# One transformer block with adaptive LayerNorm: TensorE's order in the four query blocks given as a list of 4188 single decisions instead of thirteen rules named by a table

## The chip, the cores and the metric

The kernel runs on one core of a Trainium2 chip. Its time is the device time of one execution in microseconds (us). A core has five engines, each with its own list of instructions that it works through in order: TensorE (PE in the profile, with PEld for the loading of its weights), VectorE (DVE), ScalarE (ACT), GpSimd (POOL) and SyncE (SP), which here issues the DMAs. An engine waits where an operand isn't there yet or where the buffer that it is to write is still being read.

## The reference

One transformer block over 2048 tokens of width 576, in float32: a conditioning vector gives six vectors that scale, shift and gate two LayerNorms and their branches; attention has 32 heads of 18, the MLP a hidden width of 4608.

```python
mod = (_silu(c) @ w_mod).reshape(c.shape[0], 6, 1, -1)
sa, ca, ga, sb, cb, gb = (mod[:, 0], mod[:, 1], mod[:, 2], mod[:, 3], mod[:, 4], mod[:, 5])
h = _layernorm(x, axis=-1) * (1 + ca) + sa
x = x + ga * _A_ref(h, A_wqkv, A_wo)
h = _layernorm(x, axis=-1) * (1 + cb) + sb
x = x + gb * _B_ref(h, B_w1, B_w2)
...
scores = jnp.einsum("bhqd,bhkd->bhqk", q, k) * (Dh ** -0.5)
p = _softmax(scores, axis=-1)
o = jnp.einsum("bhqk,bhkd->bhqd", p, v)
...
h = _silu(jnp.einsum("bsd,df->bsf", x, w1))
out = jnp.einsum("bsf,fd->bsd", h, w2)
```

## The kernel before, in words

**Stages.** A first part (up to some 155 us of the span) normalizes x, transposes it and computes all values and the first queries and keys. Then come four blocks of 512 queries. A block goes through the 32 heads in eight groups of four ("quads"), a quad through 16 tiles of 128 keys. What follows the attention of a block (output projection, second LayerNorm, the MLP) is computed while the next block's attention runs; that of the last block stands alone at the end (the tail).

**Three kinds of steps.** TensorE's order between the first part and the tail is a sequence of steps of three kinds, and the whole change is about that sequence:

- A *score step* (`s`, slot_a L835 and slot_b L865) is two matmuls of 512 columns that use one half of the array's rows each and run side by side. `psa` (L831, q·k with the queries in the rows) serves for the maximum of each row of scores: DVE reduces it (`mx`, L833). `psb` (L883, k·q with the keys in the rows) belongs to a place 40 slots earlier, whose maximum is known by then; ACT takes its exp into a tile `pt` (L885). Three banks of PSUM serve `psa` (and one more that it may borrow from the filler as long as the MLP isn't open), three `psb` in block 0 and two later. A bank is free again when DVE or ACT has read it.
- A *value step* (`1` to `4`, run_pv L905, pv L913) multiplies the exps of one to four tiles of keys with the values. A tile of keys is four matmuls (one for each head), each on 32 columns of the array, and each goes through the array in two passes, so that the profile shows 8 records of L920 for one tile. All 16 tiles of a quad add up in the one bank `psv`; then ACT copies it out (`ov`, L924), DVE transposes and divides by the sums (L938 to L943), and DMAs bring it to `ou` (L948). Nine `pt` pairs exist, so scores can run only so far ahead of the values.
- A *filler step* (`f`, Filler L287) is a piece of other work. In block 0 it is five (or four) matmuls over all 128 rows that compute the rest of the queries and keys (`psqk`, L612), then the filler list is empty until the block's attention is done. Then, for the block that has just ended: the projection (`psp`, from the split copies `th` and `tl` of `ou`, L1007 to L1012), the LayerNorm, the transposes `psT` (L1071), and the MLP, where `w1t` goes with `hh`/`hl` (mlp1, L1141) and `w2t` with `g` (mlp2, L1174). These are float32 products made of parts (hi·hi, hi·lo, lo·hi), split into pairs of half-row matmuls (L499); in the tail they go over all rows (L493). Between mlp1 and mlp2 stand ACT's tanh (L1167), DVE (L1168), ACT's `g` (L1170) and POOL's low part of `g` (L1171).

So the array is used in three shapes: half rows, all rows, 32 columns.

**The end of a block.** The projection of a block may start when its last quad's values are out, transposed, moved by DMA and split (`th`). The last group of mlp2 of the MLP that runs beside it (the last four of the 36 hidden tiles, `left` in the code) is kept back to be done there.

**What sets the order.** A planner (Plan, L113) follows the kernel while it is built: it has a clock `plan.t`, adds the cost of each step of TensorE (a score step TS, a tile of values TV, TX for a change of the array's shape, L93), and works off queues for DVE and ACT with their durations, so that it knows at each point which banks would be free. The main loop (L1613) asks at each point which kinds of step would be ready by that plan, and takes one of them by nine numbers (how far the filler may be ahead or behind its pace, how many tiles of values are collected, how loaded DVE must be, ...). Thirteen such rules have letters (WAYS, L61), and a table of letters (TABLE, L77) names one for every six half slots. Where no step is taken, the plan's clock moves on by 20 ns. All decisions fall when the kernel is built; the chip gets a fixed list. What the steps issue on SP (loads of `ka`, `kb`, `qt`, `vt`, of weights, stores) is issued with the step; weights of block 0's MLP are loaded raw, split by POOL (L720 to L724) and stored, paced by the plan's clock (serve, L733). The order on DVE, ACT and POOL is set by a scheduler that works from the same program.

Of the kernel before, what the change touches and what calls it, by code (L numbers as in the profile page):

```python
# [39 lines left out]
LEAD = 40  # L40
# [20 lines left out]
WAYS = {  # L61
# [13 lines left out]
}  # L75
SPAN = 6
TABLE = (  # L77
    "aaaaaaaaaaaaaaaaaaaaaaakaaaakgaaaaakaaaaaaaaaaaaaaaaaaaamaaaaaaaaaacaaaaaaaaakaaaaaaaaaaaaaaaaaaaaad"
    "aggaaaggaaaaaaaaaaaaaaaaaaaaaaaaaaaaaaaaaaaaaaaaaaaaaaaaaaaaaaaaaaaaaaaaaaaaaaaaaaaaaaaaaaaaaeaaaamd"
    "afaaaaaaaaaaaaaaaaaafaaaaacaaaaamaaaaaaaaaaaaaaaaaaaaaaaaaaaaaaaaaaafmalaaaafammfaada"  # L80
# [12 lines left out]
TS, TV, TX, TL, TR = 229, 862, 112, 430, 60  # L93
# [260 lines left out]
def tile_adaln_block(ctx: ExitStack, tc: tile.TileContext, x, wqkv, wo, w1, w2, c, wfirst, wcol, out):  # L354
# [1257 lines left out]
    stood = 0  # L1612
    while now < 2 * (total + LEAD) or pend or later:  # L1613
# [8 lines left out]
        more = now < 2 * (total + LEAD)  # L1622
        n = kts_ready()
        room = state["p"] + (now % 2 == 0) <= len(pts)
        scores = more and room and plan.is_ready(plan.when("b")) and (plan.is_ready(plan.when("a")) or may_borrow())
        work = fill.pos < len(fill.items)
        AHEAD, KEEP, NEAR, LOADED, LOADED2, NEXT, STAND, PVMAX, PVMIN = WAYS[TABLE[min(now // SPAN, len(TABLE) - 1)]]
        target = fill.target() if work else now + AHEAD - 1
        ahead = now - target
        busy = work and fill.ready()  # L1630
        if n >= PVMAX or n and more and not room and (ahead < 0 or not busy):
            do = "v"
        elif "p" not in mp:

            if busy and plan.mode != "half" and ahead > -NEXT and plan.backlog("V") >= LOADED2:
                do = "f"
            elif scores and ahead < AHEAD:
                do = "s"
# [99 lines left out]
```

## Time and profile before

| | us |
|---|---|
| three runs: median (lowest to highest) | 2374.59 (2371.91 to 2375.4) |
| the profiled execution | 2372.1 |
| its span, first to last instruction | 2370.3 |
| block 0: first psb to first psp | 155.6 to 569.2 |
| block 1: first psp to first psp of the next | 569.2 to 1105.0 |
| block 2 | 1105.0 to 1615.1 |
| block 3, up to its first psp | 1615.1 to 2108.3 |
| tail, to the end of the span | 2108.3 to 2370.3 |

The mean granted clock of TensorE is 0.991 of full speed. In the profile a group has its source line, engine, operation and tiles (out<-in), the number of instructions, their busy time and mean duration, and the idle time of the engine before them with what ended it. Rows in order of time have start, duration, the same names, and idle time in brackets.

### The profile page before, as it was taken

The page shows a single profiled execution, that of the slowest core. Times are in us where ns is not written, and L with a number is a line of the kernel's source. Part 1 is how long each engine was busy: PE and PEld are TensorE (multiplying, and loading weights), DVE is VectorE, ACT ScalarE, POOL GpSimd, SP SyncE. Part 2 cuts the span into 40 slices and gives each one's busy share as a digit, 9 for nine tenths or more (in the row PEclk, how much of TensorE's full clock was granted, in tenths as well). Part 3 has the DMA queues.
Part 4 walks back from the last instruction along what each step waited for, and adds up shares of the span by engine and source line. Part 5 has one row for each costly group of instructions (what it writes and reads, how often), then busy time and mean ns, then how long its engine had stood idle before and what let it go on. Part 6 is the DMA issues. An engine that isn't in the chain of part 4 may idle for free.

```text
span 2370.3 us, 52177 instructions
## 1 busy us (share of the span) xinstructions
PE 2301.3 (97%) x19844; PEld 1576.1 (66%) x19844; DVE 1775.2 (75%) x3089; ACT 1476.4 (62%) x2710; POOL 710.1 (30%) x873
## 2 busy tenths in 40 slices
PE   5999999999999999999999999999999999989999
PEld 4874444445566677666667776766666777678998
DVE  7768989887888888777888878887888888144333
ACT  4237777775677777666777777775777777712121
POOL 5104333316656666664211111122211111110000
PEclk9999999999999999999999999999999999999999
DMA  7455546546656666665655445554545554335653
GB/s 248 158 184 177 177 155 175 176 161 198 207 181 219 214 215 215 215 211 177 227 168 178 165 165 180 175 187 143 192 163 189 179 188 155 113 138 205 217 204 115
DMA packets 201475, 433.02 MB, mean 183 GB/s; under 512 B 31362, under 2 KB 67618, under 8 KB 201226
## 3 DMA queue, kind: packets, MB, share of 16 engines
q1 hardware_dynamic: 201226, 429.68, 54.6%
q8 instruction: 159, 2.61, 0.5%
q14 instruction: 90, 0.74, 0.1%
HBM read 338.54 MB, written 86.33 MB: 179 GB/s over the span
## 4 chain that ended last, share of the span: by engine, by line
PE 85%; DVE 6%; DMA 3%; POOL 2%; ACT 1%; issue 1%; SPq 0%; DVEq 0%; ACTq 0%; POOLq 0%
PE ps L499 25%; PE psv L920 18%; PE psa L831 13%; PE ps L493 10%; PE psb L883 8%; PE psqk L612 4%; DVE mx L833 3%; PE psv L499 2%; PE psp L499 1%; DMA raw<-in_w 1%; PE psv L1400 1%; PE psqk L499 1%; PE psqk L1400 1%; PE psp L493 1%; DMA kb<-kscr 1%
## 5 line engine op out<-in xcount | busy, mean ns | idle before, releaser
L833 DVE TENSOR_REDUCE mx<-psa 128x1 f32<-128x512 f32 x2048 | 1329.0, 684 | 287.2 <-PE psb L883 164.2
L885 ACT ACTIVATE pt<-psb 128x512 f32<-128x512 f32 x2048 | 1139.9, 599 | 472.9 <-PE psb L883 299.8
L883 PE MATMUL psb<-qt,kb 56*128 56x512 f32 x2048 | 738.9, 421 | 6.4 <-ACT pt L885 5.6
L831 PE MATMUL psa<-ka,qt 54*128 54x512 f32 x2016 | 724.0, 418 | 8.0 <-DVE mx L833 6.3
L831 PEld LDWEIGHTS psa<-ka,qt 54*128 54x128 f32 x2016 | 340.2, 186 | 306.5 <-DVE mx L833 204.9
L920 PE MATMUL psv<-pt,vt 128*32 128x512 f32 x4096 | 509.7, 602 | 0.2 <-ACT ov L924 0.2
L499 PE MATMUL ps<-w2t,g 64*128 64x288 f32 x4992 | 406.2, 294 | 8.5 <-POOL w2t L724 5.7
L499 PEld LDWEIGHTS ps<-w2t,g 64*128 64x128 f32 x4992 | 381.0, 186 | 41.8 <-POOL w2t L724 7.0
L883 PEld LDWEIGHTS psb<-qt,kb 56*128 56x128 f32 x2048 | 346.8, 186 | 35.1 <-ACT pt L885 24.1
L499 PE MATMUL ps<-hh,w1t 64*128 64x512 f32 x1944 | 358.0, 394 | 1.6 <-DVE x L1033 1.5
L1171 POOL TENSOR_TENSOR g<-etmp,g 128x512 fp32r<-128x512 f32 x108 | 137.4, 1292 | 406.3 <-ACT g L1170 298.5
L920 PEld LDWEIGHTS psv<-pt,vt 128*32 128x32 f32 x4096 | 101.0, 109 | 214.7 <-issue 209.4
L499 PEld LDWEIGHTS ps<-hh,w1t 64*128 64x128 f32 x1944 | 196.7, 187 | 45.0 <-DVE mx L833 5.0
L1037 POOL TENSOR_TENSOR x<-x,gt 128x288 f32<-128x288 f32 x116 | 93.0, 802 | 402.0 <-ACT gt L1036 401.5
L499 PE MATMUL ps<-hl,w1t 64*128 64x512 f32 x864 | 179.4, 392 | 0.0
L1033 DVE TENSOR_TENSOR x<-ps,x 128x288 f32<-128x288 f32 x184 | 83.7, 455 | 113.6 <-PE ps L493 76.8
L493 PE MATMUL ps<-w2t,g 128*128 128x288 f32 x960 | 133.2, 299 | 7.4 <-ACT g L1170 5.9
L493 PEld LDWEIGHTS ps<-w2t,g 128*128 128x128 f32 x960 | 130.8, 191 | 9.9 <-ACT g L1170 6.3
L1167 ACT ACTIVATE eq<-ps 128x512 f32<-128x512 f32 x36 | 21.5, 598 | 146.4 <-PE ps L493 146.4
L493 PE MATMUL ps<-hh,w1t 128*128 128x512 f32 x360 | 107.0, 391 | 0.5 <-DVE hh L428 0.5
L499 PEld LDWEIGHTS ps<-hl,w1t 64*128 64x128 f32 x864 | 90.1, 187 | 14.8
L1168 DVE SCALAR_TENSOR_TENSOR etmp<-etmp 128x512 f32<-128x512 f32 x108 | 75.8, 739 | 27.7 <-ACT etmp L1167 27.5
(150 smaller groups left out, 2124.7 us busy)
## 6 DMA issues: line engine op xcount, KB each, us to landing
w1t<-w1s SPq DMA_DIRECT2D x108, 640.0 KB
w2t<-w2s SPq DMA_DIRECT2D x108, 576.0 KB
kb<-kscr SPq DMA_DIRECT2D x512, 108.0 KB
ka<-kscr SPq DMA_DIRECT2D x504, 108.0 KB
w1s<-w1t SPq DMA_DIRECT2D x36, 640.0 KB
w2s<-w2t SPq DMA_DIRECT2D x36, 576.0 KB
vt<-vscr SPq DMA_DIRECT2D x32, 608.0 KB
qt<-qscr SPq DMA_DIRECT2D x128, 108.0 KB
```

The lines of the kernel that those rows point to most:

```text
L493: mm(self.ps[late], lhsT=lhsT, rhs=rhs, start=(i == 0), stop=(i == self.n - 1))
L499: done = mm(self.ps[g], lhsT=lhsT[rows], rhs=rhs[rows], start=(s == 0), stop=(s == self.end))
L612: mm(qk_ps[0], lhsT=w[b][:, kt, :], rhs=(hTl if a else hTh)[:, kt, n * 512:(n + 1) * 512], start=(i == 0), stop=(i == 13))
L831: mm(ps, lhsT=t["q"][64 * j:64 * j + 54, hp, stt * P:(stt + 1) * P], rhs=t["a" if ("a", kc, hp) in t else "b", kc, hp][64 * j:64 * j + 54, ...
L833: return lambda: nc.vector.tensor_reduce(t["mx"][:, 2 * j + hp, stt, kc:kc + 1], ps, axis=AX.X, op=ALU.max)
L883: state["pe"] = mm(ps, lhsT=t["b", kt // 4, hp][64 * e:64 * e + 56, kt % 4 * P:(kt % 4 + 1) * P], rhs=t["q"][64 * e:64 * e + 56, hp, :], s ...
L885: nc.scalar.activation(t["P"][kt, hp][:, e, :], ps, AF.Exp, scale=SCALE)
L920: mm(t["ps"][32 * h:32 * h + 32, :], lhsT=t["v"][:, c0:c0 + 32], rhs=t["P"][kt, h // 2][:, h % 2, :], start=(kt == 0), stop=(kt == NKT - 1 ...
L1033: nc.vector.tensor_add(c["x1"][j][:, hs], ps, c["x1"][j][:, hs])
L1037: nc.gpsimd.tensor_add(c["x1"][j][:, hs], c["x1"][j][:, hs], t)
L1168: nc.vector.scalar_tensor_tensor(t, t, 1.0, u, op0=ALU.add, op1=ALU.mult)
L1171: (nc.vector if last else nc.gpsimd).tensor_tensor(g[:, 1, :], t, f(g[:, 0, :]), op=ALU.subtract)
```

## The change

The table of rules and the thirteen rules go. In their place stands a string with one character for each step: `s`, `f`, or a digit for a value step of so many tiles. The main loop takes the next character and waits, by the plan's clock, until that step is ready by the plan; it never takes another one. The planner's costs for a score step, a tile of values and a change of shape become smaller. The instructions themselves stay what they are.

```diff
-WAYS = {
-    "a": (12, 6, 500, 900, 900, 8, 0, 5, 3),
...
-SPAN = 6
-TABLE = (
-    "aaaaaaaaaaaaaaaaaaaaaaakaaaakgaaaaakaaaaaaaaaaaaaaaaaaaamaaaaaaaaaacaaaaaaaaakaaaaaaaaaaaaaaaaaaaaad"
...
+ORDER = (
+    "sssfsssfsssfsss1sss1sssfsssfsssfss1sss1sss1sss1sss1sss1sss1sss2sssfsssfsssfsss1sss1sss1sss1ss1sssfsss2sssffsss"
...
-TS, TV, TX, TL, TR = 229, 862, 112, 430, 60
+TS, TV, TX, TL, TR = 228, 858, 100, 430, 60
...
         room = state["p"] + (now % 2 == 0) <= len(pts)
-        scores = more and room and plan.is_ready(plan.when("b")) and (plan.is_ready(plan.when("a")) or may_borrow())
-        work = fill.pos < len(fill.items)
-        AHEAD, KEEP, NEAR, LOADED, LOADED2, NEXT, STAND, PVMAX, PVMIN = WAYS[TABLE[min(now // SPAN, len(TABLE) - 1)]]
-        target = fill.target() if work else now + AHEAD - 1
-        ahead = now - target
-        busy = work and fill.ready()
-        if n >= PVMAX or n and more and not room and (ahead < 0 or not busy):
-            do = "v"
...
-        elif n >= PVMIN or n and stood >= STAND:
-            do = "v"
+        do = ORDER[step] if step < len(ORDER) else ""
+        if do == "s":
+            ready_ = room and plan.is_ready(plan.when("b")) and (plan.is_ready(plan.when("a")) or may_borrow())
+        elif do == "f":
+            ready_ = fill.pos < len(fill.items) and fill.ready()
         else:
-            do = None
-        stood = 0 if do else stood + 20
-        if not do:
-            if not more and not pend:
+            ready_ = do and kts_ready() >= int(do)
+        if not ready_:
+            if not do and not pend:
                 run_later(2)
                 state["now"] += 1
                 now += 1
             plan.t += 20
             continue
+        step += 1
```

What this moves on TensorE is shown at three places. The line numbers of the changed kernel are 20 higher: L851 is the `psa` of L831, L903 the `psb` of L883, L940 the values of L920, L519 and L513 the filler of L499 and L493. `psa` and `psb` one after the other are one score step; two rows of `psv` with their x2 are one tile of keys.

The first place is TensorE at the end of block 0, behind the last `psqk`, where there is no filler until the projection. Before:

```order
L920 MATMUL psv_6441<-pt_2034,vt_2040 32x512 x2
L920 MATMUL psv_6441<-pt_2035,vt_2040 32x512 x2
L831 MATMUL psa<-ka_82,qt 128x512
L883 MATMUL psb<-qt,kb_85 128x512
L831 MATMUL psa<-ka_82,qt 128x512
L883 MATMUL psb<-qt,kb_85 128x512
L831 MATMUL psa<-ka_82,qt 128x512
L883 MATMUL psb<-qt,kb_84 128x512
L831 MATMUL psa<-ka_82,qt 128x512
L883 MATMUL psb<-qt,kb_84 128x512
L920 MATMUL psv_6441<-pt_2036,vt_2040 32x512 x2
L920 MATMUL psv_6441<-pt_2037,vt_2040 32x512 x2
```

At the same place in the changed kernel:

```order
L940 MATMUL psv_6475<-pt_2036,vt_2040 32x512 x2
L940 MATMUL psv_6475<-pt_2037,vt_2040 32x512 x2
L851 MATMUL psa<-ka_80,qt 128x512
L903 MATMUL psb<-qt,kb_87 128x512
L851 MATMUL psa<-ka_80,qt 128x512
L903 MATMUL psb<-qt,kb_87 128x512
L940 MATMUL psv_6475<-pt_2038,vt_2040 32x512 x2
L940 MATMUL psv_6475<-pt_2030,vt_2040 32x512 x2
```

Four score steps stood between two tiles of values; now two do, at most of these places, and once twelve. The last `psqk` stands 59 score steps ahead of the first `psp` before, and 47 now.

The second place is TensorE at the end of block 1, behind the last matmuls of mlp1 (`w1t` with `hh`, whose result `g` the first w2t matmul behind it needs). Before:

```order
L499 MATMUL ps_15173<-hh,w1t 128x512
L920 MATMUL psv_15400<-pt_2038,vt_2039 32x512 x2
L920 MATMUL psv_15400<-pt_2030,vt_2039 32x512 x2
L831 MATMUL psa<-ka_83,qt 128x512
L883 MATMUL psb<-qt,kb_86 128x512
L831 MATMUL psa<-ka_83,qt 128x512
L883 MATMUL psb<-qt,kb_86 128x512
L920 MATMUL psv_15400<-pt_2031,vt_2039 32x512 x2
L920 MATMUL psv_15400<-pt_2032,vt_2039 32x512 x2
```

At the same place in the changed kernel:

```order
L519 MATMUL ps_15263<-hh,w1t 128x512
L851 MATMUL psa<-ka_80,qt 128x512
L903 MATMUL psb<-qt,kb_88 128x512
L851 MATMUL psa<-ka_80,qt 128x512
L903 MATMUL psb<-qt,kb_88 128x512
L940 MATMUL psv_15462<-pt_2038,vt_2039 32x512 x2
L940 MATMUL psv_15462<-pt_2030,vt_2039 32x512 x2
L940 MATMUL psv_15462<-pt_2031,vt_2039 32x512 x2
L940 MATMUL psv_15462<-pt_2032,vt_2039 32x512 x2
```

From there to the first w2t matmul stood ten score steps and four tiles of values; now nine score steps and six tiles do. In addition 26 half matmuls of w1t that stood ahead of the block's last value product now stand behind it (54 at the end of block 2).

The third place is TensorE at the end of the last block's attention. Before, the last tile of values stands here, w2t halves follow, then a whole pair of mlp1 (`ps_30801` and `ps_30802`, 54 halves) up to the full-row matmuls of the tail:

```order
L499 MATMUL ps_30731<-w2t,g 128x288
L920 MATMUL psv_30198<-pt_2035,vt_2040 32x512 x2
L920 MATMUL psv_30198<-pt_2036,vt_2040 32x512 x2
L499 MATMUL ps_30730<-w2t,g 128x288
L499 MATMUL ps_30731<-w2t,g 128x288
```

At the same place in the changed kernel, behind the last matmul of that pair of mlp1:

```order
L519 MATMUL ps_30756<-hh,w1t 128x512
L940 MATMUL psv_30283<-pt_2038,vt_2040 32x512 x2
L940 MATMUL psv_30283<-pt_2030,vt_2040 32x512 x2
L940 MATMUL psv_30283<-pt_2031,vt_2040 32x512 x2
L940 MATMUL psv_30283<-pt_2032,vt_2040 32x512 x2
L940 MATMUL psv_30283<-pt_2033,vt_2040 32x512 x2
L940 MATMUL psv_30283<-pt_2034,vt_2040 32x512 x2
L940 MATMUL psv_30283<-pt_2035,vt_2040 32x512 x2
L940 MATMUL psv_30283<-pt_2036,vt_2040 32x512 x2
L513 MATMUL ps_30910<-w2t,g 128x288 x12
```

The mlp1 pair and the 24 w2t halves stood behind the last tile of values; they now stand ahead of the last four.

More of the change, by code (lines that the diff above doesn't have):

```diff
@@ L1611, in tile_adaln_block @@
     fill.pace(now, NQUAD * 64 - END0)
-    stood = 0
+    step = 0
     while now < 2 * (total + LEAD) or pend or later:
@@ L1668, in tile_adaln_block @@
             continue
-        if do == "v":
+        step += 1
+        if do == "f":
+            fill.one()
+        elif do != "s":
             run_later(1)
-            run_pv(n)
-        elif do == "f":
-            fill.one()
+            run_pv(int(do))
         else:
```

66 lines of the change are left out of this document (38 added, 28 removed), and 12 rows, old and new, of the table WAYS.

## The prediction

> **What bounds the kernel now.** I read the page first, then TensorE's rows in order of time, then stretches of the span.
>
> ```profile
> PE 2301.3 (97%) x19844; PEld 1576.1 (66%) x19844; DVE 1775.2 (75%) x3089; ACT 1476.4 (62%) x2710; POOL 710.1 (30%) x873
> L833 DVE TENSOR_REDUCE mx<-psa 128x1 f32<-128x512 f32 x2048 | 1329.0, 684 | 287.2 <-PE psb L883 164.2
> L885 ACT ACTIVATE pt<-psb 128x512 f32<-128x512 f32 x2048 | 1139.9, 599 | 472.9 <-PE psb L883 299.8
> L883 PE MATMUL psb<-qt,kb 56*128 56x512 f32 x2048 | 738.9, 421 | 6.4 <-ACT pt L885 5.6 <-DMA kb<-kscr 0.3 <-DMA vt<-vscr 0.2
> L831 PE MATMUL psa<-ka,qt 54*128 54x512 f32 x2016 | 724.0, 418 | 8.0 <-DVE mx L833 6.3
> ```
>
> TensorE is busy for 97% of the span, no other engine for more than 75%. The number of matmuls is the same in both programs, so an order can win only what TensorE spends between them. The busy figure hides that: a record lasts some 0.4 us while the next one starts 0.23 us later. So I read starts, not durations.
>
> ```profile
> 424.81 0.50 PE L612 MATMUL psqk<-hTl,wqh 128*128 128x512 f32 x1
> 425.15 0.40 PE L612 MATMUL psqk<-hTh,wqh 128*128 128x512 f32 x1
> 425.38 0.39 PE L612 MATMUL psqk<-hTh,wql 128*128 128x512 f32 x1
> ...
> 425.85 0.40 PE L612 MATMUL psqk<-hTh,wqh 128*128 128x512 f32 x1
> 426.17 0.49 PE L831 MATMUL psa<-ka,qt 54*128 54x512 f32 x1
> ...
> 426.51 0.63 PE L831 MATMUL psa<-ka,qt 54*128 54x512 f32 x2
> 426.75 0.39 PE L883 MATMUL psb<-qt,kb 56*128 56x512 f32 x1
> 427.07 1.06 PE L920 MATMUL psv<-pt,vt 128*32 128x512 f32 x8
> 428.06 0.50 PE L831 MATMUL psa<-ka,qt 54*128 54x512 f32 x1
> ...
> 428.41 0.40 PE L831 MATMUL psa<-ka,qt 54*128 54x512 f32 x1
> ...
> 430.31 0.39 PE L831 MATMUL psa<-ka,qt 54*128 54x512 f32 x1
> ...
> 430.63 0.51 PE L612 MATMUL psqk<-hTh,wql 128*128 128x512 f32 x1
> ```
>
> Three shapes of the array alternate here: half rows (scores, and the later filler in pairs), all rows (psqk), and 32 columns (psv, value products). Within a shape 512 columns go every 0.23 to 0.24 us (425.15 to 425.38, 426.51 to 426.75). Where the shape changes, the next start is late, and so is the one after it: from psqk to psa 0.32, then 0.34; from psa to psv 0.32; from psa to psqk 0.32, and behind that change 0.34 (424.81 to 425.15).
>
> ```profile
> 1203.43 0.40 PE L831 MATMUL psa<-ka,qt 54*128 54x512 f32 x1
> ...
> 1203.99 1.92 PE L920 MATMUL psv<-pt,vt 128*32 128x512 f32 x16
> 1205.84 0.50 PE L831 MATMUL psa<-ka,qt 54*128 54x512 f32 x1
> ```
>
> Two key tiles of value products take 1.85 (1203.99 to 1205.84), one takes 0.99 (427.07 to 428.06): 0.86 each and 0.13 for the change back; behind it the second pair is 0.11 late (428.06 to 428.41 against 0.24). So a **turn to value products** and back costs 0.09 + 0.13 + 0.11, about 0.34 us with the rounding, and a **turn to all rows** 0.09 + 0.11 + 0.09 + 0.11, about 0.41. The rest of TensorE's loss is waiting, and it sits at the ends of the query blocks:
>
> ```profile
> 523.60:569.20 45.60, 42.41 (x237) 16.07 (x235) 38.03 (x66) 33.04 (x63) 26.24 (x38) 1.00 0.69 228
> 1077.60:1105.00 27.40, 25.22 (x196) 13.29 (x188) 19.33 (x30) 16.79 (x33) 11.76 (x12) 0.81 0.61 210
> 1592.60:1615.10 22.50, 21.69 (x200) 11.54 (x192) 18.09 (x30) 16.26 (x32) 9.28 (x8) 1.00 0.51 166
> 1083.00:1091.00 8.00, 6.57 (x21) 2.58 (x22) 6.38 (x10) 4.90 (x10) 4.66 (x4) 0.61 0.86 286
> 1091.00:1095.00 4.00, 4.00 (x21) 1.90 (x22) 2.91 (x4) 2.24 (x5) 1.28 (x1) 0.50 0.48 160
> ```
>
> Columns: stretch, its length, busy time of PE, PEld, DVE, ACT and POOL, granted clock, DMA. The first runs from the last psqk of block 0 to the first projection (psp), the next two from the last value product of blocks 1 and 2 to theirs. Their 20 to 30 us hold few matmuls. At the end of block 1 the clock falls too: 0.61, then 0.50, some 10 us at half speed ((1 − 0.61)/0.5 × 8 + 4).
>
> **The change, part by part.** It moves matmuls and, with them, what DVE, ACT, POOL and SP do for them; it adds and removes none. The planner's three constants are in no instruction; with the order given they only shift the planned times by which weights are loaded and stored, which I cost at nothing (their cover is named below). The sum is made against the profiled execution: 2372.1 us (span 2370.3), which is 2.5 below the median of the three runs, 2374.6.
>
> *Turns.* Counted through TensorE's list from the first to the last psb: turns to value products 320 before, 309 after; turns to all rows 77 before, 67 after; direct passages between the two, which save part of a turn, 10 and 8 and left out. 11 × 0.34 + 10 × 0.41 = **7.8 us less**. These cost time on the bounding engine wherever nothing waits; where DVE is late they only fill its wait, so 4 is the low end. The Trainium skill, "TensorEngine Tiling (Array Packing)", section "Key Properties", says that a change of tiling mode drains TensorE. By one drain for each change, the first late start alone, the turns would be 0.22 and 0.18 and the sum 4.2; the rows show the second start late as well, so I keep 7.8.
>
> *End of block 0.* After the last psqk there is no filler until psp may start.
>
> ```profile
> 531.92 1.07 PE L920 MATMUL psv<-pt,vt 128*32 128x512 f32 x8
> ...
> 534.14 0.50 PE L883 MATMUL psb<-qt,kb 56*128 56x512 f32 x1 [0.24 <-ACT pt L885]
> ...
> 535.06 1.07 PE L920 MATMUL psv<-pt,vt 128*32 128x512 f32 x8
> 602.45 2.47 DVE mx L833 x4
> ```
>
> One cycle of four score steps and one value tile takes 3.14 (531.92 to 535.06), though its work is 4 × 0.23 + 0.86 + 0.34 = 2.1: the fourth step waits for ACT's exp to give back a bank. The stretch holds 59 steps, 15 value tiles and 15 turns: 13.7 + 12.9 + 5.1 = 31.7 of 45.6, so 14 us of waiting. The change keeps psqk until later and leaves 47 steps and 14 value tiles, two steps before most of them. At the old rate of waiting that is 14 × 47/59 = 11, a gain of 3. The other end is DVE: 47 maxima at 2.47/4 = 0.62 are 29 us against 27.6 of TensorE's work, so at least 1.5 of waiting, a gain of 12.5. Two steps and one value tile (1.7) cover two maxima (1.24), but twelve steps in a row do not; I take the middle, **7 less**.
>
> *Ends of blocks 1 and 2.* Before, TensorE had 20 steps, 6 and 7 value tiles in 6 turns, and 96 half matmuls of w2t to do in these stretches: 4.6 + 5.2 + 2.0 + 6.4 = 18.2 us and 19.1 (a w2t pair 0.133, from 12 rows in 0.79 below). The waits were 9.2 of 27.4 and 3.4 of 22.5. The second length shows that the chain behind the stretch (value bank out, transposes, DMA, th) needs 22.5 at most. After, 26 and 54 half matmuls of w1t, 6 steps and 2 value tiles move into it: 24.9 and 27.9 us of work. That covers the chain, and the wait for g (below) is filled with five and six value tiles instead of four and more scores. **6.5 less** in block 1 (0 if the stretch merely grows by the work moved, 9.2 at most) and **2.5** in block 2 (0 to 3.4).
>
> ```profile
> 1202.64 0.96 PE L499 MATMUL ps<-w2t,g 64*128 64x288 f32 x12
> ```
>
> The Trainium skill, "TensorE: Matmul & The Clock Gate", section "Part 1: The HAM clock gate", has the clock fall after an idle window of about 3.4 us. In the rows above it fell while TensorE was shown busy for 6.57 of 8 us, with gaps below that, so here the rows decide: thin work is enough. Its loss is within the 9.2.
>
> *The last block's end.*
>
> ```profile
> 2081.04 1.07 PE L920 MATMUL psv<-pt,vt 128*32 128x512 f32 x8
> 2082.04 1.86 PE L499 MATMUL ps<-w2t,g 64*128 64x288 f32 x24
> 2085.44 0.81 PE L499 MATMUL ps<-hh,w1t 64*128 64x512 f32 x4 [1.54 <-DVE x L1033]
> 2092.36 0.60 ACT L1160 ACTIVATE etmp<-ps 128x512 f32<-128x512 f32 x1 [7.92 <-PE ps L499]
> 2092.86 2.70 ACT L1007 ACTIVATE th<-ou 128x512 fp32r<-128x512 f32 x5
> 2099.00 0.85 PE L493 MATMUL ps<-w2t,g 128*128 128x288 f32 x2 [4.93 <-ACT g L1170]
> 2108.27 0.43 PE L493 MATMUL psp<-wo,th 128*128 128x288 f32 x2
> ```
>
> The last value product ends its issue at 2082.04, psp starts at 2108.27: 26.2 us, in which TensorE still has a whole pair of w1t to do and then waits for its g. The change does that pair before four value tiles: 24 w2t and 54 w1t halves leave the stretch, 12 × 0.133 + 27 × 0.23 = 7.8 us of work. If only they left, 18.4 would remain and nothing be won. The chain sets the floor: th is complete at 2095.56, 13.5 after the value product. g takes 15.9 from the last w1t matmul (2092.36 to 2108.27, with 48 matmuls of w2t in it), and 3.8 of that now lie under the four value tiles: 12.1. So 13.5 to 18.4; the nearer row is the chain's, **5 less** (0 to 5).
>
> All else (the blocks' middles, the start up to the first psb, the last MLP) I cost at nothing. A moved step takes with it what it issues: on SP a score step its ka, kb, qt and vt loads and a filler step its weights and stores, on POOL the splitting of w2t. The loads' cover is the lead of many steps that they have: TensorE waited 0.3 us for kb and 0.2 for vt in all (psb's row above). POOL's cover is thinner (w2t's row below). If that cover goes, or if the small waits go, it is by about what the three largest groups show together, 22.9 us: psb 6.4, psa 8.0 and w2t 8.5:
>
> ```profile
> L499 PE MATMUL ps<-w2t,g 64*128 64x288 f32 x4992 | 406.2, 294 | 8.5 <-POOL w2t L724 5.7 <-POOL w2t L721 2.7
> ```
>
> Sum: 7.8 + 7 + 6.5 + 2.5 + 5 = 28.8, so 2343.3 for an execution like the profiled one and **2345.8** for the median.
>
> **The rivals.**
>
> *Only turns and the last end pay.* The waits at the block ends move rather than go: twelve steps in a row leave TensorE with 12 × 0.23 = 2.8 of work in 12 × 0.62 = 7.4 us, and thin work brought the clock to half at 1091. Then 7.8 + 5 = 12.8 is won: 2361.8. For it: these stretches have waited in every block; against: their work now exceeds the 22.5 us of the chain in two of three.
>
> *More goes.* The 22.9 us of small waits also go: 51.7, 2322.9. For it: 14.4 of them are psa and psb waiting for a bank, which groups of three steps spread evenly. Against: POOL's w2t, 8.5 of it, isn't touched.
>
> *Nothing comes out.* The list holds each place at which TensorE waits as firmly as the rules did; 28.8 us won are lost to waits at new places. 2374.6.
>
> *Slower: value products wait for their exps.* One mechanism: TensorE works in order, and each of 310 runs of value products stands behind the last exp of its tile. Queued behind it are the next scores, and for these wait DVE and ACT. If a run comes half an exp earlier than ACT can follow (599 ns, the page's row), it costs 0.3 × 310 = 93 us: 2374.6 + 93 − 28.8 = 2439. It turns the sign from 28.8/310 = 0.093 us a run. Against it: before, no wait of psv for pt is among the rows of waits, and runs of four tiles (31 instead of 6) ask for exps that are older on the whole. For it: single runs rise from 185 to 206.
>
> That the change does not do what it says is no case here: the two lists differ as described, and all matmuls are in both.
>
> **How the numbers follow.** Forecast 0.57, only turns 0.20, more 0.08, nothing 0.08, slower 0.07. What this kernel's measurement can tell from no change is about 0.2%, 4.7 us. Faster by more: 0.57 + 0.20 + 0.08 = 0.85; within: 0.08; slower: 0.07. The range leaves out nothing and slower (0.15), and reaches from the case of more, rounded down, to the case of turns alone with 5 us of margin for its unknown small waits: 2322 to 2367.
>
> **What would show it.** Turns: 11 and 10 fewer, each at 0.34 and 0.41 in rows of starts. Block 0: psqk's last record to psp's first, 45.6 before, near 35 (27.6 of work and 7). Block 1: the stretch from psv's last to psp's first is near 26 with a clock of 1.00 where it had 27.4 with more than 8 us less work in 0.81. Last end: psv to psp 13.5 to 16 instead of 26.2, and no 4.93 before L493. Wrong would be: psv rows with pt as releaser, w2t's 8.5 grown to 20 or more, or a clock near 0.5 in block 0's stretch.

## The result, and the profile after

| | before | after |
|---|---|---|
| median of four runs (lowest to highest), us | 2373.25 (2371.3 to 2375.4) | 2357.82 (2354.75 to 2358.8) |
| after : before, with 95% interval | | 0.993 (0.9918 to 0.9943) |
| the profiled execution; its span | 2372.1; 2370.3 | 2358.8; 2356.2 |
| granted clock | 0.991 | 0.990 |

The change makes the kernel 0.7% faster: 15.4 us between the medians, 14.1 between the spans. Of the 28.8 us forecast, half came; 2357.8 lies within 2322 to 2367. One execution of e4 below, its profiled one, was a slow one (2756.8 us at a granted clock of 0.75): it is left out of e4's median, and no row of e4 is read. The page of after, with engines first and then groups (busy time, mean ns | idle time before them and what ended it):

```profile
PE 2286.8 (97%) x19844; PEld 1579.9 (67%) x19844; DVE 1775.4 (75%) x3089; ACT 1470.7 (62%) x2710; POOL 711.9 (30%) x873
L903 PE MATMUL psb<-qt,kb 56*128 56x512 f32 x2048 | 740.0, 421 | 2.8 <-ACT pt L905 2.8
L851 PE MATMUL psa<-ka,qt 54*128 54x512 f32 x2016 | 729.6, 418 | 10.8 <-DVE mx L853 8.4
L519 PE MATMUL ps<-w2t,g 64*128 64x288 f32 x4992 | 407.3, 292 | 2.5 <-POOL w2t L744 1.7
L519 PE MATMUL ps<-hh,w1t 64*128 64x512 f32 x1944 | 360.8, 396 | 8.0 <-POOL w1t L743 5.4
```

The last of these rows in before:

```profile
L499 PE MATMUL ps<-hh,w1t 64*128 64x512 f32 x1944 | 358.0, 394 | 1.6 <-DVE x L1033 1.5
```

The same work on every engine. The small waits moved: psb's fell from 6.4 to 2.8 us and w2t's from 8.5 to 2.5, psa's rose from 8.0 to 10.8, and w1t's from 1.6 to 8.0, now for POOL. To see all of it I gave every start of TensorE its price in both traces (a pair of scores 0.232 us, a pair of w2t halves 0.133, a tile of values 0.858, the turns as the prediction has them), and called the rest of the distance to the next start waiting. This counts a halved clock as waiting too. From the first psb to the end, in us, worked out from some 19,000 rows each (a half slot is the place of one score step; they are counted through the list, and a block of queries has 512):

```
                                        before          after
                                     turns  waits    turns  waits
block 0, up to the last psqk                   13.8           18.9
  last psqk to first psp                       14.7           10.8
  first psp to the projection's last            5.5           10.6
  from there to the first w1t                   5.4            8.4
  first w1t to half slot 720                    3.7           13.8
block 1 (half slots 720 to 1104)               17.9            8.6
  its end (1104 to 1232)                       12.5            6.5
block 2, and its end                     4.8 + 7.9      3.4 + 5.7
block 3                                         2.5            3.8
tail (from half slot 2128)                     17.4            9.5
sum                                  139.8    106.1   131.8   100.1
```

The turns fell by 8.0. The waits fell at every place that the prediction named, by 20.0 together (3.9 + 6.0 + 2.2 + 7.9). But 18.2 came back in one place that it had costed at nothing: block 0 behind its first psp (14.0 and 14.4 in e8 and e10 below, whose order is the same there). The windows of after (stretch, its length, busy time of PE, PEld, DVE, ACT, POOL, clock, DMA) have the last psqk to the first psp first, then the three pieces behind it, then the ends of blocks 1 and 2 from the last value product to psp:

```profile
533.80:572.40 38.60, 36.67 (x207) 13.85 (x208) 31.40 (x55) 27.34 (x50) 22.27 (x32) 0.91 0.67 223
572.40:603.90 31.50, 25.59 (x274) 20.88 (x272) 17.68 (x42) 11.06 (x21) 18.40 (x28) 0.89 0.44 147
603.90:622.00 18.10, 13.14 (x79) 6.16 (x75) 13.79 (x30) 7.43 (x12) 14.99 (x22) 0.72 0.46 127
622.00:703.80 81.80, 74.61 (x660) 54.46 (x659) 60.35 (x97) 51.83 (x94) 42.67 (x57) 0.92 0.58 199
1081.70:1109.40 27.70, 26.57 (x242) 15.49 (x240) 22.04 (x35) 19.96 (x38) 19.41 (x22) 1.00 0.73 242
1584.50:1613.90 29.40, 29.01 (x268) 18.59 (x266) 21.43 (x35) 20.22 (x38) 10.20 (x9) 1.00 0.60 211
```

The same three pieces in before, from 569.1 us:

```profile
569.10:596.80 27.70, 24.69 (x279) 19.99 (x281) 18.43 (x48) 10.71 (x22) 16.01 (x27) 0.94 0.46 147
596.80:615.00 18.20, 16.30 (x96) 7.03 (x96) 15.60 (x33) 11.43 (x21) 15.74 (x23) 0.91 0.56 194
615.00:686.70 71.70, 71.03 (x640) 47.49 (x640) 60.55 (x101) 52.39 (x97) 37.55 (x49) 1.00 0.60 198
```

Length times (1 − clock) is the most that a halved clock can have taken (where TensorE stands it takes nothing). Up to psp that is 3.5 us in after and 0 in before (as the prediction's window shows); behind psp it is 3.5 + 5.1 + 6.5 = 15.1 in after and 1.7 + 1.6 = 3.3 in before. So up to 11.8 of the 18.2 is clock. What TensorE stopped for ahead of it, in after from 540 to 710 us (total, times, longest):

```profile
PE ps L519 <- POOL w1t L743: 5.4, 2, 4.2
PE psT L1091 <- DVE ob L435: 4.9, 1, 4.9
PE psa L851 <- DVE mx L853: 3.7, 2, 2.8
PE psp L519 <- POOL tl L1030: 2.5, 2, 2.3
PE ps L519 <- POOL w1t L744: 1.8, 2, 1.2
```

POOL's splits, and the LayerNorm's chain: 2.8 of psa's 3.7 came while DVE stood in that chain (`ob` is the LayerNorm's output). POOL's rows (start, duration, names, idle time before) and one of DVE show how the two hang together:

```profile
549.36 2.31 POOL L740 TENSOR_TENSOR raw<-raw,ga 128x288 f32<-128x288 f32 x3 [12.80 <-DMA x<-in_x]
...
590.08 1.57 POOL L740 TENSOR_TENSOR raw<-raw,gb 128x288 f32<-128x288 f32 x2
...
593.88 0.81 POOL L1057 TENSOR_TENSOR x<-x,gt 128x288 f32<-128x288 f32 x1
```

```profile
594.71 0.46 DVE L1063 BATCH_NORM_STATS2 st<-x 128x6 f32<-128x288 f32 x1 [2.24 <-POOL x L1057]
```

POOL begins to split wo at 549.4 us, 15.9 after the last psqk's start at 533.4: the kernel opens the MLP, and asks for wo, only when its list of fillers is empty. Later its addition for the LayerNorm waits behind 4 us of w2t, and DVE waits for that. Before has the same queue, from 579.95 to 583.75 us, and DVE waits there too:

```profile
584.58 0.46 DVE L1043 BATCH_NORM_STATS2 st<-x 128x6 f32<-128x288 f32 x1 [1.78 <-POOL x L1037]
```

So that queue by itself is not what is new; new are the waits for tl, for w1t and the longer one for ob (1.6 us in before).

### The profile page after: what moved, and what is told of

It is laid out like the page before. It is cut to its first block, busy times and chain, and to the rows that moved or that the text cites. A ratio compares the mean times of both kernels' runs of the same rounds, so it can differ in the third digit from the quotient of the medians.

```text
span 2356.2 us, 52136 instructions
## 1 busy us (share of the span) xinstructions
PE 2286.8 (97%) x19844; PEld 1579.9 (67%) x19844; DVE 1775.4 (75%) x3089; ACT 1470.7 (62%) x2710; POOL 711.9 (30%) x873
## 4 chain that ended last, share of the span: by engine, by line
PE 85%; DVE 6%; DMA 3%; POOL 2%; issue 1%; ACT 1%; SPq 0%; ACTq 0%; DVEq 0%; POOLq 0%
PE ps L519 26%; PE psv L940 18%; PE psa L851 14%; PE ps L513 10%; PE psb L903 8%; PE psqk L632 3%; DVE mx L853 3%; PE psv L519 2%; PE psp L519 1%; PE psqk L519 1%; PE psv L1420 1%; PE psqk L1420 1%; PE psp L513 1%; DMA vt<-vscr 1%; DMA raw<-in_w 1%
## 5 line engine op out<-in xcount | busy, mean ns | idle before, releaser
L903 PE MATMUL psb<-qt,kb 56*128 56x512 f32 x2048 | 740.0, 421 | 2.8 <-ACT pt L905 2.8
L851 PE MATMUL psa<-ka,qt 54*128 54x512 f32 x2016 | 729.6, 418 | 10.8 <-DVE mx L853 8.4
L851 PEld LDWEIGHTS psa<-ka,qt 54*128 54x128 f32 x2016 | 344.5, 186 | 314.2 <-DVE mx L853 200.9
L940 PE MATMUL psv<-pt,vt 128*32 128x512 f32 x4096 | 505.2, 601 | 0.0
L519 PE MATMUL ps<-w2t,g 64*128 64x288 f32 x4992 | 407.3, 292 | 2.5 <-POOL w2t L744 1.7
L519 PEld LDWEIGHTS ps<-w2t,g 64*128 64x128 f32 x4992 | 383.4, 185 | 30.9 <-ACT etmp L1187 2.5
L519 PE MATMUL ps<-hh,w1t 64*128 64x512 f32 x1944 | 360.8, 396 | 8.0 <-POOL w1t L743 5.4
L903 PEld LDWEIGHTS psb<-qt,kb 56*128 56x128 f32 x2048 | 350.3, 186 | 24.3 <-ACT pt L905 12.8
L940 PEld LDWEIGHTS psv<-pt,vt 128*32 128x32 f32 x4096 | 102.0, 109 | 207.5 <-issue 201.2
L519 PEld LDWEIGHTS ps<-hh,w1t 64*128 64x128 f32 x1944 | 200.4, 188 | 52.3 <-POOL w1t L743 6.3
L519 PE MATMUL ps<-hl,w1t 64*128 64x512 f32 x864 | 181.6, 394 | 0.0
L513 PE MATMUL ps<-w2t,g 128*128 128x288 f32 x960 | 130.8, 296 | 2.9 <-POOL g L1191 1.4
L513 PEld LDWEIGHTS ps<-w2t,g 128*128 128x128 f32 x960 | 128.6, 188 | 5.6 <-POOL g L1191 1.9
L513 PE MATMUL ps<-hh,w1t 128*128 128x512 f32 x360 | 106.9, 390 | 0.5 <-DVE hh L448 0.5
L519 PEld LDWEIGHTS ps<-hl,w1t 64*128 64x128 f32 x864 | 91.4, 188 | 15.7
```

Source lines behind the costliest of these rows:

```text
L513: mm(self.ps[late], lhsT=lhsT, rhs=rhs, start=(i == 0), stop=(i == self.n - 1))
L519: done = mm(self.ps[g], lhsT=lhsT[rows], rhs=rhs[rows], start=(s == 0), stop=(s == self.end))
L851: mm(ps, lhsT=t["q"][64 * j:64 * j + 54, hp, stt * P:(stt + 1) * P], rhs=t["a" if ("a", kc, hp) in t else "b", kc, hp][64 * j:64 * j + 54, ...
L903: state["pe"] = mm(ps, lhsT=t["b", kt // 4, hp][64 * e:64 * e + 56, kt % 4 * P:(kt % 4 + 1) * P], rhs=t["q"][64 * e:64 * e + 56, hp, :], s ...
L940: mm(t["ps"][32 * h:32 * h + 32, :], lhsT=t["v"][:, c0:c0 + 32], rhs=t["P"][kt, h // 2][:, h % 2, :], start=(kt == 0), stop=(kt == NKT - 1 ...
```

## The experiments

The theory at first: holding psqk back opens the MLP later, so POOL is late, and TensorE waits. Rivals: the order behind (half slots 586 to 644) is itself at fault; thin work halves the clock. Each ratio is to executions of before made beside that kernel. The waits are those of the table above, in its four indented places.

| kernel | median | ratio (95% interval) | psqk to psp | projection | to w1t | to 720 |
|---|---|---|---|---|---|---|
| before | 2373.25 | | 14.7 | 5.5 | 5.4 | 3.7 |
| after | 2357.82 | 0.9930 (0.9918 to 0.9943) | 10.8 | 10.6 | 8.4 | 13.8 |
| e1 psqk early | 2359.80 | 0.9932 (0.9909 to 0.9955) | 19.1 | 7.7 | 5.9 | 11.2 |
| e2 old head | 2345.29 | 0.9875 (0.9855 to 0.9895) | 14.7 | 6.5 | 9.5 | 0.6 |
| e3 old, psqk late | 2393.34 | 1.0074 (1.0051 to 1.0097) | 9.3 | 23.3 | 8.4 | 2.8 |
| e4 no gate of wo | 2354.63 | 0.9918 (0.9896 to 0.9940) | | | | |
| e5 old head, new seam | 2360.53 | 0.9937 (0.9913 to 0.9961) | 20.7 | 8.0 | 5.9 | 11.1 |
| e6 new head, old seam | 2355.36 | 0.9917 (0.9891 to 0.9944) | 7.4 | 21.0 | 9.2 | 1.6 |
| e7 spread | 2359.49 | 0.9933 (0.9907 to 0.9959) | 11.4 | 13.8 | 6.8 | 15.1 |
| e8 old tail | 2362.02 | 0.9944 (0.9928 to 0.9960) | 12.1 | 12.0 | 5.8 | 10.8 |
| e9 cover | 2341.28 | 0.9854 (0.9839 to 0.9869) | 14.7 | 5.5 | 3.5 | 4.8 |
| e10 turns | 2362.48 | 0.9946 (0.9929 to 0.9962) | 12.4 | 8.8 | 6.4 | 13.8 |
| e11 no gates | 2343.37 | 0.9863 (0.9849 to 0.9878) | 12.1 | 2.7 | 4.1 | 13.5 |
| e12 later mlp1 | 2352.36 | 0.9908 (0.9891 to 0.9924) | 12.1 | 6.9 | 9.7 | 8.6 |

After, e8 and e10 have the same order up to half slot 1686 at least; their four waits add up to 43.6, 40.7 and 41.4, single ones differ by up to 3.2. What is smaller than that is not read there. From half slot 1616 to the end, eight other kernels with after's order take the same time within 0.4 us.

### psqk early in after (e1), and late in before (e3)

```diff
 ORDER of after, from half slot 542
-fsss2sssffsss1sss1sss1sssfsssfsss1sss1sss1ssssfs
+ffsss2fssss1ssfsssffsss1ssss1sssss1ssss1ssss1sss
```

> The order of after with six filler steps of psqk moved forward, so that the last stands at half slot 554 (as before) and not at 576; eight tiles of values around them are put between the scores anew, all behind the place is as in after. Late-opening theory (the MLP's pools open, and POOL's splitting of wo begins, only when the filler list is empty, and 22 half slots later POOL's chain makes TensorE wait through the projection, the LayerNorm and the first w1t): POOL begins its first wo multiply at least 8 us earlier relative to the last psqk's old place, the waits between 545 and 655 us fall from some 41 to 20 to 28 us, of which 3 to 5 come back where psqk no longer covers DVE: 2340 to 2350. Rival (the waits come from the composition of the stretch, twelve scores in a row and single tiles, or from DVE's LayerNorm order): within 3 us of after, 2355 to 2361.

Nothing was won, as the rival said. POOL did begin early, and was no longer the one that TensorE waited for at psp; it even stood idle there (start, duration, names, idle time before):

```profile
539.22 2.31 POOL L740 TENSOR_TENSOR raw<-raw,ga 128x288 f32<-128x288 f32 x3 [12.46 <-DMA raw<-in_wo]
...
578.27 1.16 POOL L1024 CAST th<-ou 128x512 fp32r<-128x512 f32 x2 [9.68 <-PE psb L903]
```

The pieces behind psp fell by 8.0 (10.6 + 8.4 + 13.8 to 7.7 + 5.9 + 11.2), of which 3 may be scatter, and the stretch without filler, now 69 score steps long, took 8.3 back. And 11.2 of the last piece stayed: opening is not the only cause.

```diff
 ORDER of before, from half slot 554 (constants of before)
-fss1ss1ssss1ssss1ssss1ssss1sss
+ss1ss1ssss1ssss1ssss1ssss1ssfs
```

> The order of before with one single character moved: the last filler step of psqk (four matmuls) from half slot 554 to 576, with the old constants. Late-opening theory: POOL's splitting of wo starts some 15 us later, th is complete late, and TensorE waits 8 to 20 us more between the end of block 0 and the first mlp1: 2381 to 2394. Rival (it is not the opening): one filler step more in the uncovered stretch, 2370 to 2376, that is no change or a little faster than before.

One character, four matmuls, 18 us (before ran in 2375.07 beside it). TensorE waits at psp for POOL's wo (its line numbers are one lower):

```profile
PE psp L518 <- POOL wo L740: 8.6, 3, 5.4
...
PE psp L518 <- POOL wo L743: 3.3, 4, 1.2
```

So in before's order the late opening alone costs 18 us; how much it costs hangs on when psp stands in the list.

### Old head, new seam, and the four combinations (e2, e5, e6)

Both lists have done the same number of steps of each kind at half slots 586 and 644, so they can be joined there. "Head" is what lies ahead of 586 (psqk's last step at 554 in before, 576 in after), "seam" 586 to 644 (projection, LayerNorm, start of mlp1).

```diff
 ORDER from half slot 586: after's seam, and before's as in e2 and e6
-ssssssssssss1ss1ss1ss1fss1fss1ss1ssss1ssssssfffs1ssffsfsffffssfff
+1ssss1ssss1ssfffss1ssss1ssss1sffsss1sssfffffffssfffffffss1fffffff
```

> The decisions of before up to half slot 644 (all of block 0, its projection, LayerNorm and the first mlp1), those of after from there on; both lists have done the same numbers of scores, fillers and tiles there. If the loss sits in after's block 0 and its end (waits 62.4 against 43.1 us up to half slot 720), and the gains behind do not depend on it: after minus some 17, 2336 to 2346. Rival (what after wins in blocks 1 to 3 rests on what its block 0 left, such as weights split earlier): 2353 or more.

> The decisions of before up to half slot 586 (last psqk at 554, so the MLP opens early), those of after from there on (twelve scores in a row, projection, LayerNorm and first mlp1 in after's order). The run before this one with psqk early in after's own order had won nothing, so now the theory is that the loss sits in after's order between half slots 586 and 644, whose thin places bring the clock to half: 2354 to 2362, like after, with some 15 us of lost clock between 540 and 660 us. Late-opening theory: 2343 to 2349, like the kernel that takes before's order up to half slot 644.

> The decisions of after up to half slot 586 (last psqk at 576, late opening), those of before from 586 to 644, those of after behind. If the order from 586 to 644 is the cause alone: 2342 to 2349. If each stretch only fits its own opening, so that before's denser one (psp seven half slots earlier) meets POOL's late th as it did when one psqk step of before was moved (18 us slower): 2358 to 2372.

The four add up to 29.3 in before, 31.3 in e2, 45.7 in e5, 39.2 in e6 and 43.6 in after. Only old with old is cheap, and it keeps all that after wins in blocks 1 to 3 and the tail (2345.29). The new seam waits behind the first w1t with either head (11.1 and 13.8), the old one never (0.6 and 1.6); the late head makes the old seam wait at psp as in e3:

```profile
PE psp L519 <- POOL wo L741: 9.6, 3, 5.9
```

So either new half alone loses 10 to 15 us against old with old (2355.36 and 2360.53 against 2345.29), and both together lose no more (2357.82): there are two causes, one in each half, their losses do not add up, and neither the first theory nor its rival is enough alone. e5 behaved as expected of the seam; e6 as expected of halves that fit each other, though it came out 2.6 us below that bracket.

### Twelve scores in a row (e7)

```diff
 ORDER of after, from half slot 578
-1ss1ss1ss1ss1ss1ssssssssssss1ss1ss1ss1fss1fss1ss1ssss1ss
+1sss1sss1sss1sss1sss1sss1sss1sss1ssfs1sfss1sss1sss1ss
```

> After with thirteen single tiles of values between half slots 578 and 614 put evenly, one behind every three scores, in place of five close together, twelve scores in a row, and eight close together. The numbers of steps and turns are the same. Theory of thin work: the twelve scores (2.8 us of matmuls in 7.4 us of DVE's maxima) go, the 4.9 us of waiting there go to under 2 and the half clock from 546 to 552.5 us (3.3 us of loss) with it; what lies behind 570 us stays: 2350 to 2355. Rival (the waiting only moves to POOL's th, which is late in any case): 2356 to 2359.

The rival's time came, 2359.49, but only part of its reason. The half clock at 546 us went, yet the stretch up to psp waits as long as before the edit (11.4 against 10.8), and not for POOL. A cycle of three scores and one tile takes 2.64 us for 1.9 of work, since the third psb waits for ACT's exp to give back a bank:

```profile
550.14 0.50 PE L851 MATMUL psa<-ka,qt 54*128 54x512 f32 x1
...
551.36 0.49 PE L903 MATMUL psb<-qt,kb 56*128 56x512 f32 x1 [0.24 <-ACT pt L905]
...
552.78 0.50 PE L851 MATMUL psa<-ka,qt 54*128 54x512 f32 x1
```

Where after has two scores and one tile, the cycle takes 1.66 (537.40 to 539.07), and that is its work. Behind psp the wait for POOL's tl grew from 2.5 to 5.3, as the rival has it:

```profile
PE psp L519 <- POOL tl L1030: 5.3, 2, 4.8
```

### POOL's load (e4, e11)

```diff
 split_half, as in e4; e11 leaves the gates of both wo and w2t out
-        if gate is not None:
+        if gate is not None and ask["key"][0] != "wo":
```

> After, without the multiplication of wo by the gate ga (ten POOL instructions of 0.80 us, 8 us, between 549 and 574 us; the output lacks that gate); the orders of TensorE, DVE and ACT are those of after. POOL-chain theory: POOL is done with th and tl up to 8 us earlier, the 7.7 us of waiting around the first psp and part of what follows go: 2343 to 2352. Rival (POOL only looks busy, the end of the values' chain or DVE bounds): 2355 to 2360.

> After without the multiplications of wo and of w2t by their gates when they are split in block 0 (ten POOL instructions of 0.80 us before the first psp, eight more up to 615 us, and the rest later; the output lacks both gates); the orders of TensorE, DVE and ACT are those of after. Theory that POOL's load is what TensorE waits for in the 41.3 us of half slots 592 to 720: the waits for th (2.5 and a half clock of 6.7 us behind it) and for w1t (7.2 and half clocks of 10 us) go or shrink, 12 to 18 us less, 2340 to 2346. Rival (the list leaves too few steps between the projection's end and the first w1t, 7 scores where before had 15, and the LayerNorm's chain of dependent steps takes its time however free POOL is): under 6 us less, 2352 to 2358.

e4 takes 2354.63; its interval and after's overlap, so the chain theory's 2343 to 2352 did not come with wo's gate alone; the rival's 2355 to 2360 is nearer. e11 gains 14.4 (2357.82 to 2343.37): the projection's waits fall from 10.6 to 2.7, those up to w1t from 8.4 to 4.1, block 1's from 8.6 to 5.3. What TensorE still waits for in e11, and its window of the projection (POOL 10.77 of 23.7 us, in after 18.40 of 31.5):

```profile
PE ps L519 <- POOL w1t L743: 4.5, 2, 3.3
PE ps L519 <- POOL w1t L744: 3.6, 2, 3.0
```

```profile
575.40:599.10 23.70, 22.36 (x276) 18.54 (x273) 18.76 (x48) 10.82 (x21) 10.77 (x18) 0.98 0.54 165
```

So POOL's load is what holds the projection and the LayerNorm in after; what the same would win in before was not measured. The wait behind the first w1t is the same with a lighter POOL (13.5 against 13.8).

### Steps ahead of the first w1t (e12, e9)

Between the projection's last matmul and the first w1t before has 15 score steps and 5 tiles, after 7 and 5. The first casts of w1t, in before (first w1t at 615.0 us) and then in after (622.0):

```profile
603.76 0.44 POOL L723 CAST w1t<-raw 128x320 fp32r<-128x320 f32 x1
606.16 0.45 POOL L723 CAST w1t<-raw 128x320 fp32r<-128x320 f32 x1 [1.21 <-DMA raw<-in_w]
```

```profile
615.18 0.45 POOL L743 CAST w1t<-raw 128x320 fp32r<-128x320 f32 x1 [0.19 <-DMA raw<-in_w]
...
624.22 0.45 POOL L743 CAST w1t<-raw 128x320 fp32r<-128x320 f32 x1
```

The second half is cast 8.9 us ahead of its first use in before, and 2.2 behind the place where TensorE stands for it in after.

```diff
 ORDER of after, from half slot 646 (e12)
-ffssffsfsffssffsfsfsfsffs3s
+ssss1ssffsffsfffsfffsfffs2fs
```

> After with the first mlp1 of block 0 begun six score steps and one tile of values later (its fourteen filler steps of half slots 646 to 656 are packed into 652 to 657); all else as in after, the late opening too. What is left open: without the gates the waits around psp and the LayerNorm went (10.6 and 8.4 us to 2.7 and 4.1), but those behind the first w1t stayed (13.8 to 13.5), so a second cause is supposed, too few steps between the projection's end and the first w1t (7 scores and 5 tiles where before had 15 and 5). If so, 1.4 + 0.9 + 0.3 = 2.6 us of work more stand there, the waits for w1t (5.4 and 1.8) fall by that or more and a half clock of 10 us is shorter or gone: waits behind the first w1t 5 to 10 us instead of 13.8, 2350 to 2354. Rival (w1t's splits stand behind TensorE's own place in the program and move later with it): 2356 to 2360.

2352.36: the wait for L743 (5.4 us in after, 5.3 and 5.8 in e8 and e10) is gone from the rows, and the last piece falls from 13.8 to 8.6, as the second cause wants (with the same order it was 10.8 in e8). The intervals of e12 and after overlap at their ends (0.9891 to 0.9924, 0.9918 to 0.9943), so the row carries this more than the time does.

```diff
 ORDER of e2, from half slot 613 (e9)
-fffffffssfffffffss1fffffffssfffffffss1fffffffssfffffffss1fffffffssfffsfsfffs2ss1ssssf
+fffffffssfffffffssffffffffffffffss1ffffffffffffffss1fffffffssfffsfsfffs2sss1ssss1sssf
```

> Before's decisions up to half slot 644 and after's behind (the fastest so far, 2345.3), with four score steps and one tile of values moved from among the projection's fillers to behind its last one, where TensorE waits for the LayerNorm's last ob (2.4 us, and then half clock for 6.6 us). Theory (that place lacks work of TensorE's own while the LayerNorm's chain of some 10 us runs on DVE and POOL): 1.8 us of work more there, waits up to half slot 720 fall by 2 to 5 us: 2340 to 2344. Rival (four more maxima on DVE at that place hold the LayerNorm up by 4 x 0.62 = 2.5 us): 2344 to 2348.

2341.28, the fastest kernel here, 0.9854 of before (0.9839 to 0.9869). The waits up to the first w1t go from 9.5 to 3.5, and up to there the clock keeps full speed. Behind it 4.2 come back (0.6 to 4.8), so the four places together gain 2.8, and the intervals of e9 and e2 overlap: better than before is shown, better than e2 is not. Its windows of the projection, of the stretch up to the first w1t, and behind it:

```profile
566.20:592.00 25.80, 22.33 (x267) 17.89 (x266) 17.91 (x44) 8.38 (x17) 17.21 (x28) 1.00 0.48 155
592.00:611.90 19.90, 18.90 (x122) 8.40 (x122) 18.74 (x40) 14.63 (x27) 16.29 (x24) 1.00 0.54 180
611.90:684.60 72.70, 70.50 (x660) 52.52 (x659) 58.57 (x96) 51.48 (x94) 39.74 (x52) 0.98 0.65 209
```

### The price of a turn (e10), and the tail (e8)

```diff
 ORDER of after, 19 places behind half slot 1686 (e10)
-3ss
+1ss2
```

> After with 19 turns to value products more, all in blocks 2 and 3 behind half slot 1686: runs of two to four tiles are split into one tile, two other steps, and the rest; the numbers of steps and tiles stay. If a turn costs 0.34 us where nothing waits: 6.5 us more between half slots 1616 and 2128, 2362 to 2366. By one late start for each change of shape (0.22): 4.2 us. Rival (the split runs take work out of places where TensorE would have waited for DVE or ACT): under 2 us.

From half slot 1616 to the end the trace grows by 5.8 us: 5.8/19 = 0.30 us a turn. By the prices it is 6.5 more of turns and 0.7 less of waiting. The medians differ by 4.7, with intervals that overlap; the trace carries this, since that stretch repeats within 0.4 us in the other kernels.

```diff
 the end of ORDER (e8)
-sfffssfffffff4
+sfffss4
```

> After with its last seven filler steps (34 half matmuls of mlp1, 4.0 us) put behind the last four tiles of values, as before had them. All else is as in after. Theory of the last block's end: g starts as late as it did but has no tiles of values to lie under, so TensorE waits for it where it did before; the values come out 4.0 us earlier, which helps nothing: 3 to 5 us more, 2360 to 2363. Rival (the values' chain to th is what bounds): faster by up to 4 us, 2354 to 2358.

The tail waits 14.6 us instead of 9.5: the first theory. The medians differ by 4.2, with intervals that overlap, so here too the trace carries it. What the tail waits for is ACT's g, 4.5 us at once (0.3 in after), and behind that its clock is 0.50 from 2082.9 to 2089.7 us.

```profile
PE ps L513 <- ACT g L1190: 4.5, 1, 4.5
```

## Why the prediction was right, and which step failed

The sum of the named terms came out right, the line "all else" did not. That the sum agrees to 0.8 us is in part luck: block 0's term is 3.1 too large and the last block's 2.9 too small. And the time lies in the range only because the range reaches up to a rival; the forecast itself is 12 us too low. Forecast and measured, in us won:

| step | forecast | measured |
|---|---|---|
| turns | 7.8 | 8.0 by count; a turn to values measured 0.30 (e10), not 0.34, so nearer 7.4 (11 x 0.30 + 10 x 0.41) |
| end of block 0, last psqk to psp | 7 | 3.9 (2.3 to 2.6 in four kernels with the same order) |
| end of block 1 | 6.5 | 6.0 |
| end of block 2 | 2.5 | 2.2 |
| last block's end | 5 | 7.9 |
| together | 28.8 | 28.0 |
| all else | 0 (±22.9) | −13.9 |

*Turns.* Both late starts count: e10's 0.30 lies above the 0.22 of the first one alone. By the prices the missing 0.04 filled waits, as the low end allowed.

*End of block 0.* The stretch is 39.0 us long, forecast near 35. The wait fell by 3.9, near the end "at the old rate of waiting" (3). Most cycles of two scores and a tile wait for nothing (1.66 us each), but the twelve scores in a row and the half clock behind them take back part of it, and spread in threes (e7) the steps wait for ACT's exp instead.

*Ends of blocks 1 and 2.* Block 1's stretch takes 27.7 us at clock 1.00 (forecast: near 26 at 1.00), block 2's 29.4, also at 1.00; 24.9 and 27.9 of that is the work forecast, so 3 and 1.5 are left to wait.

*Last block's end.* The term was sized too small. From the last value product's issue (2083.9) to psp it takes 9.0, below the floor of 13.5:

```profile
2080.32 3.64 PE L940 MATMUL psv<-pt,vt 128*32 128x512 f32 x32
2083.89 1.07 PE L513 MATMUL ps<-w2t,g 128*128 128x288 f32 x6
...
2092.88 0.42 PE L513 MATMUL psp<-wo,th 128*128 128x288 f32 x2
...
2095.62 0.66 PE L513 MATMUL psp<-wo,th 128*128 128x288 f32 x3 [1.01 <-DVE th L1032]
```

I had taken the complete th as the start of psp. psp begins with the parts of th that earlier heads fill, and only the last part waits (at 2095.62, 11.7 behind). And the 15.9 that the prediction gave to g are g only up to 2099.0; behind that before works at half clock, which the prediction did not see (0.50 from 2095.1 to 2105.4 us; in after the stretch runs at 1.00). The w2t matmuls ahead of psp, in before and then in after:

```profile
2100.35 8.08 PE L493 MATMUL ps<-w2t,g 128*128 128x288 f32 x40 [0.49 <-POOL g L1171]
```

```profile
2087.87 5.17 PE L513 MATMUL ps<-w2t,g 128*128 128x288 f32 x37 [0.56 <-POOL g L1191]
```

So some 2.5 of the 7.9 is clock. e8 shows that 5.1 of the 7.9 hang on the seven filler steps ahead of the values.

*All else.* This is the step that failed: "All else (the blocks' middles, the start up to the first psb, the last MLP) I cost at nothing". The projection, LayerNorm and first w1t of block 0 fall under it, and cost 18.2 more; up to psqk 5.1 more; block 1 gave 9.3 back, mostly w2t's splits (the group's wait fell from 8.5 to 2.5, which I had said the change doesn't touch); blocks 2 and 3 are even to 0.1. The prediction had named the cover (POOL's, "thinner") and held to nothing. What it missed is that the opening of the MLP follows the last psqk, which it counted only as a gain, and that eight score steps less stand between the projection and w1t, where TensorE then stands for POOL's w1t. e3 shows the first in before's order and e12 the second in after's; the four combinations and e1 show that undoing one alone wins little (e1, e5, e6) and undoing both wins 12.5 us (e2).

The rival "only turns and the last end pay", 2361.8, is nearer to 2357.8 than the forecast, but not by its mechanism alone: the ends of blocks 1 and 2 paid, and the twelve scores in a row, which it named, did halve the clock (below), yet spreading them won nothing (e7). No psv row waits for pt, so the slower rival fell. w2t's wait did not grow to 20; a clock near half in block 0's stretch, the third sign of a wrong forecast, did show, for 6.8 us.

What stays open: why up to the last psqk 5 us more are waited, and how much of e11's 14.4 is wo's gate and how much w2t's; e4's 3.2, not clear of noise, leaves most of it to w2t's or to the two together.

## What to carry to other kernels

A reordered list moves the moments at which other engines get their work: before crediting a gap that closes on the bounding engine, write down which event opens the next stage, and what each helper must have finished at the new place. Where two halves of an order were found together, try them crossed with the old ones: here the old head and seam with the new rest beat both kernels (e2), and with more cover at one place (e9) the gain over before was more than twice that of the change (0.9854 against 0.993). A stop of 2 to 5 us on TensorE is to be priced with the half clock that can follow it, not by its own length alone.

## What the runs showed of the hardware

The clock is granted in windows of 3.41 us. Stretches of after, each one window long:

```profile
542.65:546.06 3.41, 3.16 (x14) 1.62 (x12) 3.13 (x6) 2.92 (x6) 0.00 (x0) 1.00 0.82 227
546.06:549.47 3.41, 3.41 (x11) 2.40 (x11) 3.22 (x6) 2.65 (x5) 0.11 (x1) 0.50 0.98 356
549.47:552.89 3.42, 3.42 (x15) 0.94 (x13) 1.21 (x3) 1.16 (x3) 3.42 (x7) 0.50 0.60 203
573.37:576.78 3.41, 1.15 (x13) 0.84 (x12) 1.50 (x3) 1.27 (x3) 3.38 (x5) 1.00 0.95 331
576.78:580.19 3.41, 2.64 (x15) 1.95 (x15) 0.00 (x0) 0.00 (x0) 2.25 (x2) 0.50 0.60 232
580.19:583.61 3.42, 3.42 (x29) 3.42 (x27) 1.98 (x3) 1.68 (x3) 0.00 (x0) 0.50 0.64 199
```

A stop of 2.26 us at 574.3 was followed by 6.8 us at half clock, up to 3.4 us lost on top. In the first window, amid the twelve scores, TensorE shows 3.16 us busy, yet its six pairs are worth 6 x 0.232 = 1.4 us, 41% of the window, and the next one is at half. From 180 to 2089 us, in both traces, each of the nine windows at full clock that half speed followed held some 10 to 41% of its length in priced work. With clearly more the clock stayed, and so it did after three windows of about 40%, so no sharp threshold is shown. The Trainium skill, "TensorE: Matmul & The Clock Gate", section "Part 1: The HAM clock gate", states such a free-running window of 3413 ns, and the starts at 546.06 and 576.78 agree with it (nine windows apart); it asks for an idle window, where here one with 41% of work was enough.
